# Row maxima of 48 row blocks taken over two key blocks at a time, six maxima per projection task, and projection steps of the attention phase that take only what is over

## The chip, the cores and the metric

The kernel runs on one core of a Trainium2 chip. The metric is the device time of one execution in microseconds (us). TensorE does the matmuls, VectorE (DVE) and ScalarE (ACT) read their results from PSUM, GpSimd (POOL) takes part of the elementwise work, and SyncE (SP) issues most of the DMAs. Each engine has its own queue of instructions.

## The reference

One transformer block over 2048 tokens of 448 features, in fp32, with conditioning vectors made from `c`:

```
mod = silu(c) @ w_mod                       # six vectors: sa, ca, ga, sb, cb, gb
h = layernorm(x) * (1 + ca) + sa
q, k, v = h @ wqkv                          # 16 heads of 28
p = softmax(q k^T / sqrt(28))               # 2048 x 2048 per head
x = x + ga * ((p v) @ wo)
h = layernorm(x) * (1 + cb) + sb
x = x + gb * (gelu(layernorm(h) @ w1 + b1) @ w2 + b2)
```

The softmax needs, for every head and query row, a number near the row's maximum score. The kernel takes that maximum from a first, coarse product of q and k, apart from the exact scores.

## The kernel before

The sequence is cut in four blocks of 512 tokens, the heads in four groups `g` of four, 32 rows each. Every operand of an exact product is split into a high and a low part (`hi`, `lo`), and a product is made of the terms hi x hi, lo x hi and hi x lo.

*First phase (lines 511 to 602).* For each token block, 10 to 14 tasks, 48 in all, numbered here from 0. A q/k task (`qk_task`, line 334) makes q or k of one group for one block: eleven matmuls into a PSUM tile `pa` (two buffers, line 337), then some row maxima, then ScalarE copies the result out (line 352), splits it, and DMAs write both parts to DRAM. A v task (`v_task`, line 363) does the same for v. Between them stand the layer norm of the next block and the transposes of its chunks (`h_chunk`, line 253, in the PSUM tile `o`).

*Row maxima.* The maxima of one head (`j`), one 128-row part (`i`) of a query block (`qt`) over one key block (`cch`) are one unit of work, here "a maximum": a matmul over 32 rows into a PSUM tile `mx` (line 382), and a VectorE reduce over its 512 columns (line 388). Four of them, with different `j`, use different row groups of TensorE. There are 16 for each (g, qt, cch), 1024 in all. They stand in a list `mxq` that is kept sorted, group 1 ahead of group 0 in the first phase, and `emit_max` (line 436) takes the next ones. A task of the first phase takes `p1_n[0]` of them, four in block 0 and five later (`P1RATE`, line 542), with five buffers `mx`.

When the 64 of a (g, qt) are done, `max_fin` (line 398) reduces the four key blocks to one value, and two steps later `put` transposes it (line 404), ScalarE negates it (line 406) and a DMA (line 407) writes it into row 28 of the q tile of that unit, where k has a row of ones: so the score matmul subtracts it. A unit's scores can't start before that DMA has landed. At the end of the first phase `finish_max(0, 0)` and `tick_late(True)` see to it that this is done for unit 0 (lines 600, 601). Then the PSUM pool is closed and the second phase opens its own.

*Second phase (lines 926 to 970).* 16 units (g, qt) of 16 steps, one for each 128 keys. A step makes the scores of four heads in two halves (line 953, twelve matmuls into tiles `s`), ScalarE takes the exponential of each half (line 958), and TensorE multiplies the exponentials of the step before with v (line 919). Between the score matmuls stand three or four maxima of later units, by a budget (lines 942, 943). From unit 12 on, steps 8 to 11 of each unit also make the output projection of a finished block (`t_wo`, line 721, matmuls at line 315): "projection steps". At step 13 of unit 14, when the maxima are done, `share(1, 3)` closes the pool with three `mx` and two `s` buffers and opens one with one and three.

*Third phase.* The MLP.

Of the kernel before, what the change touches and what calls it, by code (L numbers as in the profile page):

```python
# [13 lines left out]
F32 = mybir.dt.float32  # L14
F32R = mybir.dt.float32r
AF = mybir.ActivationFunctionType
ALU = mybir.AluOpType
# [24 lines left out]
def tile_adaln_block(ctx: ExitStack, tc: tile.TileContext, x, wqkv, wo, w1, b1, w2, b2, c, w_mod, out):  # L42
# [20 lines left out]
    def slot(tag, shape, dt=F32R):  # L63
        return sb.tile(shape, dt, tag="slot_" + tag, name=nm("slot_" + tag), bufs=1)
# [17 lines left out]
    def ps_mx():  # L82
        return psp[0].tile([128, 512], F32, tag="mx", name=nm("mx"), bufs=psp[1])
# [7 lines left out]
    def f(t):  # L91
        return t.bitcast(F32)
# [173 lines left out]
        return lambda: split_chunk(k, full, hi, lo, pool, act.copy)  # L266


    sil_b = slot("d0", [CK, NC, 32], F32)
    dve.tensor_copy(sil_b, sil[:, :, None].broadcast_to([CK, NC, 32]))  # L270
    pm = ps_s()
    warm = ps_s()
# [61 lines left out]
    def qk_task(b, kind, g, done=0, begun=None):  # L334
        p, ts = begun or qk_terms(b, kind, g)
        for i in range(done, len(ts)):
            pe.matmul(p, *ts[i], start=(i == 0), stop=(i == len(ts) - 1))  # L337
        emit_max(p1_n[0])
        bias = ones_col if kind == 1 else zero_col
        if g == 0:  # L340
            tg = ("kh" if kind else "qh") + str(b)
            hi = sb.tile([128, 512], F32R, tag=tg, name=nm(tg), bufs=1)
            (kh_sb if kind else qh_sb)[(g, b)] = hi
        elif g == 1 and b < 2:

            hi = sbt("raw" if kind else "osb", [128, 512], F32R, bufs=3 if kind else 2)
            (kh_sb if kind else qh_sb)[(g, b)] = hi
        else:
            hi = sbt("hi", [128, 512], F32R, bufs=3)
        full = sbt("full", [128, 512], bufs=3)  # L350
        lo = sbt("lo", [128, 512], F32R, bufs=3)
        act.activation(full, p, AF.Identity, bias=bias)  # L352

        def split():
            (act.copy if b else dve.tensor_copy)(hi, full)
            pool.tensor_tensor(out=lo, in0=full, in1=f(hi), op=ALU.subtract)
            sl = slice(b * 512, (b + 1) * 512)
            sp.dma_start(f(dscr[kind][0][g])[:, sl], f(hi))
            sp.dma_start(f(dscr[kind][1][g])[:, sl], f(lo))

        return split

    def v_task(b, t):
        p = ps_s()
        ts = slice(t * 128, (t + 1) * 128)
        hh, hl = hT[b]
        mm_acc(p[:, :D], terms448(
            lambda k: hh(k)[:, ts], lambda k: hl(k)[:, ts], lambda k: wv[0][:, k, :], lambda k: wv[1][:, k, :],
        ))
        emit_max(p1_n[0])  # L370
        act.copy(v_sb[b][:, t, :, :DH], p[:, :D].rearrange("p (h d) -> p h d", d=DH))


    mxp = {}
    left = {}
    mxq = []

    def max_one(g, qt, cch, i, j):
        if (g, qt) not in mxp:
            mxp[(g, qt)] = sbt("mxp", [128, 4, 4, 4], bufs=6)  # L380
        m = ps_mx()
        pe.matmul(  # L382
            m,
            qh_sb[(g, qt)][32 * j : 32 * j + 32, i * 128 : (i + 1) * 128],
            kh_sb[(g, cch)][32 * j : 32 * j + 32, :],
            start=True, stop=True,
        )
        dve.tensor_reduce(out=mxp[(g, qt)][:, i, j, cch : cch + 1], in_=m, op=ALU.max, axis=AX.X)  # L388

    def load_hi(kind, g, b):  # L390
        tg = ("kh" if kind else "qh") + str(b)
# [5 lines left out]

    def max_fin(g, qt):
        m16 = sbt("m16", [128, 4, 4], bufs=2)
        dve.tensor_reduce(out=m16, in_=mxp[(g, qt)].rearrange("p i h c -> p h i c"), op=ALU.max, axis=AX.X)  # L400

        def put():
            p = ps_mx()
            pe.transpose(p[:16, :128], m16.rearrange("p h i -> p (h i)"), ident)
            r = sbt("full", [128, 512], F32R, bufs=3)[:16, :128]
            act.activation(r, p[:16, :128], AF.Copy, scale=-1.0)
            sp.dma_start(f(qst[g * NB + qt])[DH:128:32, 0, :].rearrange("j (i q) -> j i q", q=128), f(r))

        late.append([2, put, g * NB + qt])
# [21 lines left out]
    pair_no = {}  # L431


    last_j = [None]

    def emit_max(n, half=None):
        for _ in range(n):
            if not mxq:
                return
            fits = [x for x, m in enumerate(mxq[:32]) if half is None or (m[4] // 2 == half and m[4] != last_j[0])]  # L440
            g, qt, cch, i, j = mxq.pop(fits[0] if fits else 0)
            last_j[0] = j
            max_one(g, qt, cch, i, j)
            left[(g, qt)] -= 1
            pair_no[(g, cch)] = pair_no.get((g, cch), 0) + 1
            if pair_no[(g, cch)] == 16 * NB and g + 1 < NG:
                load_hi(1, g + 1, cch)
            if left[(g, qt)] == 0:
                max_fin(g, qt)
                if g + 1 < NG:  # L450
                    load_hi(0, g + 1, qt)

    p1_n = [0]

    def finish_max(g, qt):
        while left[(g, qt)] > 0:
            emit_max(1)
# [69 lines left out]
    for b in range(NB):  # L527
# [11 lines left out]
        for n, (tb, kind, g) in enumerate(tasks):  # L539
# [2 lines left out]
            p1_n[0] = P1RATE if b < 1 else P1RATE + 1  # L542
            if not more and n == len(tasks) - 1:
                p1_n[0] = 0
            if kind < 2:
                fn = qk_task(tb, kind, g, 6, firsts[n]) if b == 0 and n < 2 else qk_task(tb, kind, g)
                if g == 0:
                    fn()
                else:
                    post.append(fn)  # L550
                if kind == 1 and (g == 0 or (g == 1 and tb < 2)):
                    newq = [(g, qt, cch) for qt in range(tb + 1) for cch in range(tb + 1) if max(qt, cch) == tb]
            else:
                v_task(tb, g)
# [42 lines left out]
                fn()  # L597
        if more:
            stages = later
    finish_max(0, 0)  # L600
    tick_late(True)
    ps1_cm.__exit__(None, None, None)
# [304 lines left out]
        for d, fn in unit_end_tasks(u, o_sb):  # L907
            at(base + 1 + d, fn)

    budget = 0.0  # L910
    pend = None
    o = None
    total_pairs = len(mxq)
    rate = total_pairs / (NKT * (NU - 1) - 6)

    def av(u, kt, p, o):
        g = u // NB
# [8 lines left out]
    for u in range(NU):  # L926
        g, qt = divmod(u, NB)
        for kt in range(NKT):
            step = u * NKT + kt
            if kt == 1 and u + 1 < NU and u + 1 not in qst:  # L930
                load_q(u + 1)
            if kt == NKT - 6 and u + 1 < NU:
                finish_max(*divmod(u + 1, NB))
            tick_late()
            if u == NU - 2 and kt == NKT - 3:
                assert not mxq and not late
                share(1, 3)
            pt = slot(ptags[step % 3], [128, 4, 512], F32)
            budget += rate

            wo_step = u >= NU - NB and 8 <= kt < 12
            n = 3 if wo_step else 4 if (step % 2 == 0 and budget > -4) or budget >= 4 else 3
            n0 = 1 if n == 3 and step % 4 == 3 else 2
            budget -= n

            ks, qs = kst[(g, kt // 4)], qst[u]
            kc = slice((kt % 4) * 128, (kt % 4 + 1) * 128)
            for hf in range(2):
                s2 = ps_s2()
                for term, (kp, qp) in enumerate(((0, 0), (1, 0), (0, 1))):  # L950
                    for jj in range(2):
                        rows_ = slice(64 * hf + 32 * jj, 64 * hf + 32 * jj + 32)
                        pe.matmul(s2[:, jj, :], ks[rows_, kp, kc], qs[rows_, qp, :], start=(term == 0), stop=(term == 2))  # L953
# [4 lines left out]
                act.activation(pt[:, 2 * hf : 2 * hf + 2, :], s2, AF.Exp, scale=SCALE)  # L958
# [102 lines left out]
```

## Time and profile before

| | us |
|---|---|
| median of 3 runs (lowest, highest) | 1161.24 (1160.32, 1162.51) |
| the profiled execution | 1159.49 |
| its span, first to last instruction | 1157.4 |
| first phase: first projection matmul to first score matmul | 20.1 to 184.5 |
| second phase, from there to the last product with v | 184.5 to 859.3 |
| third phase, from there to the end | 859.3 to 1157.4 |

Times inside the trace count from the start of the span. In a row of the timeline stand start, length, engine, line, operation, output and inputs, and how many of them were merged; in brackets how long the engine sat idle before and what it waited for. A row of the windows gives, for a stretch, its length and each engine's busy time and count, then the granted TensorE clock, the DMA share and GB/s. A row of the groups gives busy time, mean ns of one, and the idle time before.

### The profile page before, as it was taken

Reading aid. Unit: us, or ns where it says so; the run is one execution under the profiler, and the core shown is the slowest. Engines: PE = TensorE matmul, PEld = TensorE weight load, DVE = VectorE, ACT = ScalarE, POOL = GpSimd, SP = SyncE. Lnnn points to the kernel's source line nnn. Section 1 sums busy time; section 2 is a strip of 40 time slices with the busy share of each in tenths; the row PEclk is TensorE's granted clock in tenths of the full one; section 3 lists DMA queues with packets and bytes.
Section 4 is the critical chain, followed back from the end, with each engine's and each line's share of the span. In section 5 each row is a group of like instructions: output and inputs, shape, how many; then the busy total and the mean of one; then the engine's idle time right before and its main releaser. Section 6 shows DMA issues by size and latency. Waiting matters only on the chain. (4 is left out here: it accounts for less than half of the span.)

```text
span 1157.4 us, 20604 instructions
## 1 busy us (share of the span) xinstructions
PE 1142.6 (99%) x8396; PEld 685.0 (59%) x8396; DVE 853.7 (74%) x1471; ACT 663.0 (57%) x807; POOL 213.8 (18%) x215
## 2 busy tenths in 40 slices
PE   8999999999999999999999999999999999999998
PEld 6667765444444444444444444545458888888887
DVE  6879888999898889888998877686438863444322
ACT  4644536778777777777777776675863221111110
POOL 2533431210000000000000011206223513223000
PEclk9999999999999999999999999999999999999999
DMA  8652353012131111221120321120323100000000
GB/s 296 201 156 98 108 194 116 29 56 67 48 96 61 56 47 38 84 75 47 50 72 20 83 84 52 34 77 8 109 69 87 50 33 1 1 33 1 32 1 33
DMA packets 50415, 81.07 MB, mean 70 GB/s; under 512 B 11512, under 2 KB 20812, under 8 KB 50320
## 3 DMA queue, kind: packets, MB, share of 16 engines
q1 hardware_dynamic: 49696, 79.01, 21.9%
q8 instruction: 66, 1.08, 0.4%
q10 hardware_dynamic: 288, 0.46, 0.1%
q0 software_dynamic: 336, 0.28, 0.1%
q14 instruction: 29, 0.24, 0.1%
HBM read 53.11 MB, written 26.35 MB: 69 GB/s over the span
## 5 line engine op out<-in xcount | busy, mean ns | idle before, releaser
L388 DVE TENSOR_REDUCE mxp<-mx 128x1 f32<-128x512 f32 x1024 | 640.3, 683 | 100.5 <-PE mx L382 93.2
L953 PE MATMUL s<-slot_b,slot_a 32*128 32x512 f32 x3072 | 380.3, 423 | 2.1 <-ACT slot_d L958 1.0
L958 ACT ACTIVATE slot_c<-s 128x1024 f32<-128x1024 f32 x342 | 331.4, 1022 | 86.5 <-PE s L953 85.1
L953 PEld LDWEIGHTS s<-slot_b,slot_a 32*128 32x128 f32 x3072 | 214.9, 183 | 240.6 <-ACT slot_c L958 138.9
L382 PE MATMUL mx<-kh,qh 32*128 32x512 f32 x960 | 300.5, 472 | 1.2 <-DVE mxp L388 0.2
L958 ACT ACTIVATE slot_d<-s 128x1024 f32<-128x1024 f32 x170 | 164.8, 1021 | 43.4 <-PE s L953 43.4
L919 PE MATMUL o<-slot_c,v 128*32 128x512 f32 x1368 | 183.1, 605 | 0.4 <-ACT osb L905 0.4
L994 ACT ACTIVATE full<-mx,b_col 128x512 f32<-128x512 f32 x56 | 38.5, 688 | 191.9 <-PE mx L315 179.7
L382 PEld LDWEIGHTS mx<-kh,qh 32*128 32x128 f32 x960 | 121.2, 182 | 27.2 <-DVE mxp L388 17.6
L997 DVE CAST hi<-full 128x512 fp32r<-128x512 f32 x56 | 25.2, 450 | 135.4 <-ACT full L994 135.4
L704 POOL TENSOR_TENSOR osb<-osb,osb 128x512 f32<-128x512 f32 x16 | 21.3, 1333 | 485.7 <-DMA osb<-drec 362.2
L919 PE MATMUL o<-slot_d,v 128*32 128x512 f32 x680 | 90.6, 605 | 0.0
L315 PE MATMUL mx<-y,slot_a 128*128 128x512 f32 x160 | 60.6, 395 | 0.0
L919 PEld LDWEIGHTS o<-slot_c,v 128*32 128x32 f32 x1368 | 27.1, 108 | 55.5 <-issue 50.8
L352 ACT ACTIVATE full<-pa,cst 128x512 f32<-128x512 f32 x32 | 22.0, 686 | 52.8 <-PE pa L337 52.8
L998 DVE TENSOR_TENSOR lo<-full,hi 128x512 fp32r<-128x512 f32 x56 | 44.1, 788 | 5.2
L315 PE MATMUL mx<-y,slot_c 128*128 128x512 f32 x152 | 47.5, 396 | 0.1
L1012 PE MATMUL s<-slot_v,lo 128*128 128x448 f32 x128 | 46.7, 365 | 0.0
L1010 PE MATMUL s<-slot_v,hi 128*128 128x448 f32 x128 | 46.6, 364 | 0.0
L315 PE MATMUL mx<-y,slot_v 128*128 128x512 f32 x112 | 39.2, 396 | 0.0
L315 PE MATMUL mx<-y,slot_b 128*128 128x512 f32 x112 | 39.0, 398 | 0.0
L337 PE MATMUL pa<-slot_c,slot_a 128*128 128x512 f32 x136 | 36.9, 405 | 0.0
(212 smaller groups left out, 1289.7 us busy)
## 6 DMA issues: line engine op xcount, KB each, us to landing
d<-lo SPq DMA_DIRECT2D x32, 256.0 KB
slot_b<-d SPq DMA_DIRECT2D x32, 256.0 KB
slot_a<-d SPq DMA_DIRECT2D x32, 256.0 KB
d<-hi SPq DMA_DIRECT2D x20, 256.0 KB
osb<-drec SPq DMA_DIRECT2D x15, 256.0 KB
out_dram<-xn SPq DMA_DIRECT2D x16, 224.0 KB
slot_v<-in_w_mod_dram SPq DMA_DIRECT2D x4, 784.0 KB
raw<-in_B_w_dram SPq DMA_DIRECT2D x14, 224.0 KB
```

The lines of the kernel that those rows point to most:

```text
L315: pe.matmul(p, a, b, start=(i == 0), stop=(i == len(terms) - 1))
L337: pe.matmul(p, *ts[i], start=(i == 0), stop=(i == len(ts) - 1))
L382: pe.matmul(m, qh_sb[(g, qt)][32 * j : 32 * j + 32, i * 128 : (i + 1) * 128], kh_sb[(g, cch)][32 * j : 32 * j + 32, :], start=True, stop=True,
L388: dve.tensor_reduce(out=mxp[(g, qt)][:, i, j, cch : cch + 1], in_=m, op=ALU.max, axis=AX.X)
L919: pe.matmul(o[32 * j : 32 * j + 32, :], v_sb[kt // 4][:, kt % 4, 4 * g + j, :], p[:, j, :], start=(kt == 0), stop=(kt == NKT - 1),)
L953: pe.matmul(s2[:, jj, :], ks[rows_, kp, kc], qs[rows_, qp, :], start=(term == 0), stop=(term == 2))
L958: act.activation(pt[:, 2 * hf : 2 * hf + 2, :], s2, AF.Exp, scale=SCALE)
L994: act.activation(gf, p, AF.Gelu_apprx_tanh, bias=b1_col[:, i : i + 1])
L997: dve.tensor_copy(ghi, gf)
L998: dve.tensor_tensor(out=glo, in0=gf, in1=f(ghi), op=ALU.subtract)
L1010: pe.matmul(pp, ghi[:, ts], w_hi, start=(m == 0), stop=False)
L1012: pe.matmul(pp, glo[:, ts], w_hi, start=False, stop=(m == NFT - 1))
```

## The change

For the three units (0, 1), (0, 2) and (0, 3), the maxima over key blocks 0 and 1 are taken together. With a = q k0 and b = q k1, max(a, b) = a + relu(b - a), and b - a is q (k1 - k0). GpSimd makes the difference of the two k blocks once, `k_diff`. A pair is then two 32-row matmuls: one with `k_diff`, whose result ScalarE passes through a relu into a scratch in the slot `d0`, and one with k0, which VectorE adds to the scratch while it takes the maximum of the sum (`tensor_tensor_reduce`). That is 48 pairs for 96 maxima.

A task of the first phase takes one pair in blocks 0 and 1 and two in blocks 2 and 3 while there are any, puts the pair's first matmuls ahead and its second ones after two single maxima, and picks singles for the row groups that the pairs leave free. Where the tile `o` isn't needed by the task, a sixth matmul goes there.

In the second phase plain steps alternate between four and three maxima, and a projection step takes only what the plain steps left to come can't take at that rate. The pools are changed as soon as no maxima are left.

```diff
-    sil_b = slot("d0", [CK, NC, 32], F32)
+    d0 = slot("d0", [128, 4, 512], F32)
+    sil_b = d0[:CK, 0, 0 : NC * 32].rearrange("p (k r) -> p k r", r=32)
...
-        emit_max(p1_n[0])
+        emit_task(*p1_n)
...
+            if kind == 1 and (g, b) == (0, 1):
+                k_diff.append(sbt("raw", [128, 512], F32R, bufs=3))
+                pool.tensor_tensor(out=k_diff[0], in0=f(hi), in1=f(kh_sb[(0, 0)]), op=ALU.subtract)
...
+    def pair_diff(g, qt, i, j):
+        m = max_mm(g, qt, i, j, k_diff[0])
+        r = d0[:, 2 + px_no[0] % 2]
+        px_no[0] += 1
+        act.activation(r, m, AF.Relu)
+
+        def rest(ps):
+            m = max_mm(g, qt, i, j, kh_sb[(g, 0)], ps)
+            dve.tensor_tensor_reduce(
+                out=r, in0=m, in1=r, scale=1.0, scalar=-3.0e38, op0=ALU.add, op1=ALU.max,
+                accum_out=mxp[(g, qt)][:, i, j, 1:2],
+            )
+
+        return rest
...
+        if (g, qt) in paired and cch < 2:
+            if cch == 1:
+                pxq.extend((g, qt, i, j) for i in range(4) for j in range(4))
+            return
...
+    def emit_task(n, sixth, n_pairs):
+        if not n:
+            return
+        pairs = [pxq.pop(0) for _ in range(min(n_pairs, len(pxq)))]
+        rests = [pair_diff(*m) for m in pairs]
+        js = [m[3] for m in pairs]
+        n_ops = n - len(pairs) + (sixth and len(pairs) > 0)
+        singles = []
+        for x in range(n_ops - len(pairs)):
+            if mxq:
+                free = [j for j in range(4) if j not in js] or range(4)
+                fits = [y for y, m in enumerate(mxq[:32]) if m[4] == free[x % len(free)]]
+                singles.append(mxq.pop(fits[0] if fits else 0))
+        ops = [lambda ps, m=m: max_one(*m, ps) for m in singles]
+        ops[2:2] = rests
+        for x, op in enumerate(ops):
+            op(ps_o if x + len(pairs) == 5 else ps_mx)
...
+            k = n - (5 if b == 1 else 4)
+            p1_n[2] = 1 if b < 2 else 2
+            p1_n[1] = not (more and (0 <= k < NC)) and not (b == 1 and n < 4)
...
+    def is_wo(s_):
+        return s_ // NKT >= NU - NB and 8 <= s_ % NKT < 12
+
+    def left_steps(s_):
+        rest = range(s_, NKT * (NU - 1) - 6)
+        n_wo = sum(is_wo(x) for x in rest)
+        return len(rest) - n_wo, n_wo
+
+    def n_maxima(s_):
+        n_plain, n_wo = left_steps(s_)
+        over = len(mxq) - 7 * n_plain // 2
+        if is_wo(s_):
+            return max(0, -(-over // max(n_wo, 1)))
+        plain[0] += 1
+        return 4 if plain[0] % 2 or (over > 3 * n_wo and over > 0) else 3
...
-            if u == NU - 2 and kt == NKT - 3:
-                assert not mxq and not late
+            if not (three or mxq or late):
+                three = True
                 share(1, 3)
...
-            n = 3 if wo_step else 4 if (step % 2 == 0 and budget > -4) or budget >= 4 else 3
+            n = n_maxima(step)
...
-                    if hf == 0 and term < n0:
+                    if hf == 0 and term < min(n0, n):
                         emit_max(1, 1)
-                    if hf == 1 and (term == 0 or (term == 2 and n - n0 > 1)):
+                    if hf == 1 and ((term == 0 and n - n0 > 0) or (term == 2 and n - n0 > 1)):
                         emit_max(1, 0)
```

More of the change, by code (lines that the diff above doesn't have):

```diff
@@ L369, in v_task @@
         ))
-        emit_max(p1_n[0])
+        emit_task(*p1_n)
         act.copy(v_sb[b][:, t, :, :DH], p[:, :D].rearrange("p (h d) -> p h d", d=DH))
@@ L376, in tile_adaln_block, with max_mm, max_one @@
     mxq = []
-    def max_one(g, qt, cch, i, j):
+    pxq = []
+    k_diff = []
+    paired = ((0, 1), (0, 2), (0, 3))
+    px_no = [0]
+    def max_mm(g, qt, i, j, k, ps=None):
         if (g, qt) not in mxp:
             mxp[(g, qt)] = sbt("mxp", [128, 4, 4, 4], bufs=6)
[L381 to L388, printed above, removed]
+        m = (ps or ps_mx)()
+        js = slice(32 * j, 32 * j + 32)
+        pe.matmul(m, qh_sb[(g, qt)][js, i * 128 : (i + 1) * 128], k[js, :], start=True, stop=True)
+        return m
+    def max_one(g, qt, cch, i, j, ps=None):
+        m = max_mm(g, qt, i, j, kh_sb[(g, cch)], ps)
+        dve.tensor_reduce(out=mxp[(g, qt)][:, i, j, cch : cch + 1], in_=m, op=ALU.max, axis=AX.X)
+    def pair_diff(g, qt, i, j):
[10 more added lines that the diff above has]
+        return rest
     def load_hi(kind, g, b):
@@ L399, in max_fin @@
         m16 = sbt("m16", [128, 4, 4], bufs=2)
-        dve.tensor_reduce(out=m16, in_=mxp[(g, qt)].rearrange("p i h c -> p h i c"), op=ALU.max, axis=AX.X)
+        c0 = 1 if (g, qt) in paired else 0
+        dve.tensor_reduce(out=m16, in_=mxp[(g, qt)][:, :, :, c0:].rearrange("p i h c -> p h i c"), op=ALU.max, axis=AX.X)
         def put():
@@ L431, in tile_adaln_block, with count @@
     pair_no = {}
+    def count(g, qt, cchs):
+        left[(g, qt)] -= len(cchs)
+        for cch in cchs:
+            pair_no[(g, cch)] = pair_no.get((g, cch), 0) + 1
+            if pair_no[(g, cch)] == 16 * NB and g + 1 < NG:
+                load_hi(1, g + 1, cch)
+        if left[(g, qt)] == 0:
+            max_fin(g, qt)
+            if g + 1 < NG:
+                load_hi(0, g + 1, qt)
     last_j = [None]
@@ L443, in emit_max @@
             max_one(g, qt, cch, i, j)
[L444 to L453, printed above, removed]
+            count(g, qt, [cch])
+    def emit_task(n, sixth, n_pairs):
[15 more added lines that the diff above has]
+            op(ps_o if x + len(pairs) == 5 else ps_mx)
+        for g, qt, cch, i, j in singles:
+            count(g, qt, [cch])
+        for g, qt, i, j in pairs:
+            count(g, qt, [0, 1])
+    p1_n = [0, False, 1]
     def finish_max(g, qt):
@@ L599, in tile_adaln_block @@
             stages = later
+    assert not pxq
     finish_max(0, 0)
@@ L908, in end_unit @@
             at(base + 1 + d, fn)
-    budget = 0.0
     pend = None
     o = None
-    total_pairs = len(mxq)
-    rate = total_pairs / (NKT * (NU - 1) - 6)
+    plain = [0]
+    three = False
+    def is_wo(s_):
[11 more added lines that the diff above has]
+        return 4 if plain[0] % 2 or (over > 3 * n_wo and over > 0) else 3
     def av(u, kt, p, o):
@@ L934, in tile_adaln_block @@
             tick_late()
-            if u == NU - 2 and kt == NKT - 3:
-                assert not mxq and not late
+            if not (three or mxq or late):
+                three = True
                 share(1, 3)
             pt = slot(ptags[step % 3], [128, 4, 512], F32)
-            budget += rate
-            wo_step = u >= NU - NB and 8 <= kt < 12
-            n = 3 if wo_step else 4 if (step % 2 == 0 and budget > -4) or budget >= 4 else 3
+            n = n_maxima(step)
             n0 = 1 if n == 3 and step % 4 == 3 else 2
-            budget -= n
             ks, qs = kst[(g, kt // 4)], qst[u]
```

## The prediction

> **What bounds the kernel now.** I read the page first (busy time, costliest groups), then the timeline of one projection task, the windows of the first phase, the timeline of two attention steps, the windows of the steps that carry an output projection, and last the timeline of the seam between the phases.
>
> ```profile
> PE 1142.6 (99%) x8396; PEld 685.0 (59%) x8396; DVE 853.7 (74%) x1471; ACT 663.0 (57%) x807; POOL 213.8 (18%) x215
> L388 DVE TENSOR_REDUCE mxp<-mx 128x1 f32<-128x512 f32 x1024 | 640.3, 683 | 100.5 <-PE mx L382 93.2
> ```
>
> TensorE is in use from end to end and the row maxima are three quarters of VectorE's work. The whole is a string of stages, so each is priced alone. A projection task is eleven matmuls and a group of maxima (each maximum: one 32-row matmul, one reduce):
>
> ```profile
> 160.04 3.08 DVE L388 TENSOR_REDUCE mxp<-mx 128x1 f32<-128x512 f32 x5 [0.31 <-PE mx L382]
> 160.21 1.20 PE L337 MATMUL pa<-slot_c,slot_a 128*128 128x512 f32 x4
> 162.61 0.39 PE L337 MATMUL pa<-slot_c,slot_a2h 128*128 128x512 f32 x1
> 162.93 0.74 PE L382 MATMUL mx<-kh,qh 32*128 32x512 f32 x5
> 163.46 3.08 DVE L388 TENSOR_REDUCE mxp<-mx 128x1 f32<-128x512 f32 x5 [0.34 <-PE mx L382]
> 163.60 2.78 PE L337 MATMUL pa<-slot_c,slot_a 128*128 128x512 f32 x11
> ```
>
> From 160.21 to 163.60 is a task of 3.4 us. Five reduces in a row take 3.08, so one costs 0.60 start to start (683 ns is one alone). VectorE has 0.3 left: TensorE is the bound by a little. Where VectorE has other work, or TensorE waits for a transpose of finished maxima, it turns round:
>
> ```profile
> 96.94:115.22 18.28, 18.16 (x84) 12.08 (x82) 18.01 (x36) 7.30 (x12) 5.47 (x6) 1.00 0.15 58
> 143.14:167.03 23.89, 23.89 (x114) 16.45 (x113) 21.27 (x36) 8.39 (x13) 7.73 (x6) 1.00 0.51 171
> 167.03:181.35 14.32, 13.73 (x68) 9.50 (x67) 13.37 (x24) 5.30 (x10) 3.72 (x6) 1.00 0.81 256
> 142.71 0.18 PEld L382 LDWEIGHTS mx<-kh,qh 32*128 32x128 f32 x1 [0.37 <-DVE mxp L388]
> ```
>
> The columns after the length are PE, PEld, DVE, ACT, POOL. Seven quiet tasks take 23.89 (3.41 each). Tasks 23 to 27 (counted from 0), with layer-norm statistics on VectorE, take 18.28, with VectorE busy 18.01 of it. Tasks 43 to 46, a q/k task and three v tasks, take 14.32; a v task has shorter matmuls (eleven in 2.50 below against 2.78), so 3.41 + 3 x 3.1 = 12.7 would do. In the second phase:
>
> ```profile
> 399.86 0.50 PE L953 MATMUL s<-slot_b,slot_a 32*128 32x512 f32 x2
> 400.43 2.48 DVE L388 TENSOR_REDUCE mxp<-mx 128x1 f32<-128x512 f32 x4 [0.33 <-PE mx L382]
> 402.60 0.50 PE L953 MATMUL s<-slot_b,slot_a 32*128 32x512 f32 x2
> 404.81 0.50 PE L953 MATMUL s<-slot_b,slot_a 32*128 32x512 f32 x2
> ```
>
> The TensorE rows are the starts of three steps. The first step holds four maxima (four reduces, 2.48) and takes 2.74, the second holds three and takes 2.21: a maximum in a plain step costs 0.53.
>
> **The change, part by part.** The order of the built program gives the counts: 201 maxima in the first phase become 229, of which 96 are taken as 48 pairs; 823 in the second become 795.
>
> *First phase.* VectorE's maximum operations fall from 201 to 181: 133 reduces and 48 pair operations. The trace has no pair operation. The nearest row below is a plain two-input operation from PSUM, 686 ns (about 0.60 back to back, if it overlaps as a reduce does); above it twice a reduce, 1.37, if it went over its data twice. The built program holds two instructions a pair, the second writing one column, so I add part of a small instruction (182) and take 0.75.
>
> ```profile
> L803 DVE TENSOR_TENSOR y<-mx,y 128x512 fp32r<-128x512 f32 x12 | 7.9, 686 | 10.6 <-ACT y L801 10.5
> L164 DVE BATCH_NORM_AGGREGATE mv<-st 128x2 f32<-128x6 f32 x48 | 8.7, 182 | 1.6
> L801 ACT CAST y<-mx 128x512 fp32r<-128x512 f32 x13 | 7.3, 589 | 4.4 <-PE mx L240 4.4
> 115.22:136.67 21.45, 21.45 (x114) 15.64 (x113) 18.44 (x31) 13.43 (x24) 11.41 (x11) 1.00 0.45 148
> ```
>
> The Trainium skill ("VectorE: DVE Perf Modes", section on two Vector instructions with no wait between them) says that an operation with an accumulator output is a main instruction and an accumulator read; it gives no price for the read, and no run so far shows one.
>
> A group of six has no more passes over TensorE than one of five, since the order puts at most two in one row group: nothing. Task 13 goes from four to five: +0.2, one matmul of 512 columns. Tasks 23 to 27: 25 reduces (15.0) become 16 reduces and 7 pair operations (9.6 + 5.25 = 14.85), and the last two tasks end with less left on VectorE; between nothing and 0.6, I take -0.3. Task 35: its wait of 0.37 goes, -0.4. Tasks 43 to 46: two reduces and two pairs are 2.7, under 3.1, and the two transposes of finished maxima are no longer there: 12.7 for 14.32, -1.6. The relus are 48 x 0.59 = 28 us of ScalarE. It is fullest in tasks 28 to 33, busy 13.43 of 21.45; with twelve relus, 20.5. That just fits under the matmuls; without that cover it costs up to 0.3 a task, some 2 us. The extra subtraction on GpSimd (1.3, k block 1 less k block 0) stands two tasks ahead of its first reader. Sum **-2.1**.
>
> *The seam.* Unit 0's maxima are now finished after the last task: the order shows nine maxima of (0, 0) after its matmuls, and only then the last reduce, the transpose, the copy and the DMA that carry the maxima into the q tile which the first score matmul reads. Before, that DMA was issued tasks earlier.
>
> ```profile
> 139.58 5.58 DVE L388 TENSOR_REDUCE mxp<-mx 128x1 f32<-128x512 f32 x9 [0.37 <-PE mx L382]
> L400 DVE TENSOR_REDUCE m<-mxp 128x16 f32<-128x64 f32 x16 | 3.5, 220 | 0.6
> 181.32 0.28 PE L404 MATMUL mx<-ident,m 128*16 128x128 f32 x1 [0.27 <-DVE mxp L388]
> 181.35 2.52 PE L315 MATMUL pa<-slot_e,slot_c 128*128 128x448 f32 x11
> 181.69 0.27 ACT L406 ACTIVATE full<-mx 16x128 fp32r<-16x128 f32 x1 [1.02 <-PE mx L404]
> 181.98 0.55 SPq L407 DMA_DIRECT2D slot_b<-full  x1
> 184.49 0.50 PE L953 MATMUL s<-slot_b,slot_a 32*128 32x512 f32 x2 [0.62 <-ACT v L371]
> 818.76 0.55 SPq L689 DMA_DIRECT2D den<-osb  x1
> 820.63 0.25 DVE L695 RECIPROCAL rec<-den 128x16 f32<-128x16 f32 x1 [5.36 <-DMA den<-osb]
> ```
>
> On the clock of this trace: the last projection matmul starts at 183.5 (181.35 + 2.52 - 0.37); the maxima 0.32 later (162.61 to 162.93), VectorE 0.53 after that, 184.35. Nine reduces 5.58: 189.9. Last reduce 0.14 beyond (0.22 less the overlap): 190.1. Transpose to DMA issue 0.66 (181.32 to 181.98): 190.7. An 8 KB DMA from issue to its waiting reader 1.87 (818.76 to 820.63): 192.6. The first scores start there and not at 184.49: **+8.1**. Nothing covers it: no other TensorE instruction stands between in its queue. SP's reload of q for the next group stands ahead of this DMA but waits only for the ninth matmul, some 3.7 earlier.
>
> *Second phase.* Seven of the 28 leave plain steps (one each in units 3, 7 and 10, two each in 12 and 13): 7 x 0.53 = **-3.7**. The other 21 leave projection steps: 7, 8 and 6 in units 12, 13 and 14.
>
> ```profile
> 685.87:703.61 17.74, 3.67 (x12) 1.60 (x12) 1.00 0.00 1
> 734.40:755.08 20.68, 4.28 (x12) 1.96 (x12) 1.00 0.01 2
> 786.46:806.30 19.84, 3.00 (x8) 1.28 (x8) 1.00 0.01 2
> 833.82:852.17 18.35, 0.00 (x0) 0.00 (x0) 1.00 0.34 91
> 836.02 2.62 PE mx L315 x12
> 796.90 1.17 PE L953 MATMUL s<-slot_b,slot_a 32*128 32x512 f32 x12
> 801.74 1.00 PE L953 MATMUL s<-slot_b,slot_a 32*128 32x512 f32 x12
> 809.30 0.98 PE L953 MATMUL s<-slot_b,slot_a 32*128 32x512 f32 x12 [1.02 <-ACT slot_d L958]
> ```
>
> The first four rows are the windows of the four projection steps of units 12 to 15, busy times of the maxima's matmuls alone. Unit 15 has none and takes 18.35; unit 13 has twelve and takes 2.33 more (0.19 each), unit 14 eight and 1.49 more (0.19). Unit 12 projects three parts of four, 4 x 0.66 less (2.62 / 4), and is 2.0 over that (0.17). At 0.185, 21 are **-3.9** (bounds: 0.11, and 0.53 as in a plain step; the lower one because the step from 796.90 to 801.74 has no maximum among its scores and still takes 4.84, 0.25 over unit 15's mean, so that much of 0.58 a step may be unit 15's third score buffer). The change of PSUM pools now comes as soon as maxima are done, two steps earlier, in a projection step whose 2.62 us of matmuls cover the wait of 1.02 for the last exponential: **-0.9**. A transpose of maxima more, unit 1's, falls into this phase: **+0.3** (0.28).
>
> *Sum:* -2.1 + 8.1 - 3.7 - 3.9 - 0.9 + 0.3 = -2.2. The profiled execution took 1159.49 (span 1157.4 and 2.1 around it), so 1157.3 on its clock; it lies 1.75 under the median of the runs, and 1161.24 - 2.2 = **1159.0**.
>
> **Rivals.** *The pair operation is dear* (the slower side). Place: tasks of two pairs, and tasks 23 to 27. Up to 0.9 it is hidden. At x, a v task needs 1.2 + 2x against 3.1 and a q/k task against 3.4; tasks 23 to 27 pay 7 (x - 0.75). At 1.37: 0.55 x 9 q/k, 0.85 x 4 v, 4.3 in tasks 23 to 27 less 1.1 counted twice, 1.2 at the seam where VectorE is late: +13, 1172. It decides from about 1.12, where 4.5 are lost and the change is 2.3 slower than before. For it: no row of such an operation; against: 686 ns for two inputs.
>
> *The clock falls at the seam.*
>
> ```profile
> 1152.00:1154.00 2.00, 0.40 (x3) 0.03 (x1) 1.61 (x3) 0.00 (x0) 0.00 (x0) 1.00 0.59 223
> 1154.00:1157.10 3.10, 0.00 (x0) 0.00 (x0) 0.00 (x0) 0.00 (x0) 0.00 (x0) 1.00 0.40 152
> 1157.20:1157.40 0.20, 0.00 (x0) 0.00 (x0) 0.00 (x0) 0.00 (x0) 0.00 (x0) 0.50 0.00 0
> ```
>
> After the last matmul (1152.4) the granted clock held 4.7 us and then went to 0.50. At the seam the ninth matmul is done near 187.4 and scores start at 192.6: 5.2 without work but for one transpose. If it falls and stays low as long as it held here, 4.7 at half rate lose 2.3: 1161.3. Against: the transpose splits the gap into 2.7 and 2.2. The Trainium skill ("TensorE: Matmul & The Clock Gate", Part 1) has a free-running window of 3.4 us after which an idle array halves its clock; by that rule neither piece alone would do it. The trace's 4.7 agrees with one to two such windows.
>
> *Projection steps hide maxima anyway:* at 0.11 a maximum, -2.3 for -3.9: 1160.6. *VectorE's relief pays more:* a first phase without any wait for VectorE would be 1.2 shorter still in tasks 23 to 27 (18.28 against 3.41 x 4 + 3.1 = 16.7, of which 0.3 is taken above): 1157.8. *Not what it says* is excluded: the order shows 28 maxima moved.
>
> **How the numbers follow.** Forecast as summed, plus or minus 2.5: 0.48. Dear pair 0.22, fallen clock 0.13, hidden maxima 0.09, more relief 0.08. A run of this kernel tells some 0.2% (2.3 us) from no change; the forecast lies on that line, so it is halved, 0.24 faster and 0.24 within. Faster 0.24 + 0.08 = 0.32; within 0.24 + 0.13 + 0.09 = 0.46; slower 0.22. The range goes from 1155.0 (all favourable bounds but the plain-step price) to 1166.0, which takes in a fallen clock and a pair operation up to about 1.15, and leaves 0.2 out.
>
> **What would show it.** Right: the nine reduces at the seam followed by about 2.7 us without VectorE work, scores starting some 6 later than the first-phase tasks alone would have it; tasks 43 to 46 in 12.7; units 12 to 14 shorter by about 2.4, 2.5 and 2.0. Wrong: a pair of VectorE rows over 1.0 together; TensorE waiting for the relu; a granted clock under 1.00 after the seam; projection steps that keep their length.

## The result and the profile after

| | before | after |
|---|---|---|
| median, us (lowest, highest; 17 runs each) | 1161.39 (1159.93, 1164.9) | 1163.79 (1162.92, 1164.7) |
| ratio after / before, 95% interval | | 1.0016, 1.0009 to 1.0024 |
| profiled execution, its span | 1159.49, 1157.4 | 1164.21, 1162.2 |
| mean granted clock of the profiled execution | 1.00 up to the last matmul | 0.994 |

The change makes the kernel 2.4 us slower; 1159.0 was forecast. The windows of the changed kernel show it stage by stage: the first phase, three stretches of it (one with a low clock, tasks 23 to 27, tasks 43 to 46), the seam from the start of the last task to the first score matmul, the spell of low clock behind it, and the second phase. The columns after the length are PE, PEld, DVE, ACT, POOL, then the granted clock, DMA share and GB/s.

```profile
20.50:180.56 160.06, 158.21 (x806) 110.53 (x806) 122.50 (x264) 98.28 (x176) 63.36 (x61) 0.99 0.49 160
35.03:38.44 3.41, 3.41 (x10) 2.67 (x9) 2.10 (x5) 2.15 (x4) 1.42 (x2) 0.50 0.45 172
98.98:116.48 17.50, 17.50 (x88) 12.10 (x86) 16.68 (x40) 9.53 (x18) 5.07 (x5) 1.00 0.16 60
167.88:180.56 12.68, 12.68 (x71) 9.14 (x69) 10.03 (x25) 9.09 (x17) 3.92 (x7) 1.00 0.71 220
180.56:192.10 11.54, 5.74 (x23) 3.30 (x22) 8.14 (x16) 2.18 (x5) 0.00 (x0) 0.85 0.40 139
188.63:198.87 10.24, 6.78 (x40) 3.47 (x40) 5.00 (x9) 4.14 (x5) 3.14 (x4) 0.50 0.30 72
192.10:864.50 672.40, 670.42 (x6114) 311.28 (x6118) 543.25 (x902) 514.80 (x561) 84.94 (x71) 0.99 0.20 60
```

The same stretches of the kernel before:

```profile
20.13:181.35 161.22, 158.58 (x789) 110.59 (x789) 139.59 (x249) 77.29 (x131) 62.09 (x60) 1.00 0.51 165
181.35:184.49 3.14, 2.52 (x14) 1.97 (x14) 2.30 (x4) 0.80 (x2) 0.00 (x0) 1.00 0.28 91
184.49:859.32 674.83, 671.90 (x6141) 310.44 (x6145) 559.08 (x929) 514.88 (x560) 84.54 (x71) 1.00 0.20 60
```

The first phase is 1.2 shorter, although task 5 ran at half clock; the second phase is 2.4 shorter, although it began at half clock; the seam takes 11.54 for 3.14, 8.4 more than before, and that is more than both gains. The timeline of the seam:

```profile
180.56 2.49 PE L317 MATMUL pa<-slot_e,slot_c 128*128 128x448 f32 x11
183.51 5.47 DVE L397 TENSOR_REDUCE mxp<-mx 128x1 f32<-128x512 f32 x9 [0.51 <-PE mx L392]
189.02 0.22 DVE L427 TENSOR_REDUCE m<-mxp 128x16 f32<-128x64 f32 x1
189.29 0.38 PE L431 MATMUL mx<-ident,m 128*16 128x128 f32 x1 [2.75 <-DVE m L427]
189.77 0.27 ACT L433 ACTIVATE full<-mx 16x128 fp32r<-16x128 f32 x1 [6.15 <-PE mx L431]
190.06 0.62 SPq L434 DMA_DIRECT2D slot_b<-full  x1
192.10 0.79 PE L1030 MATMUL s<-slot_b,slot_a 32*128 32x512 f32 x2 [2.43 <-DMA slot_b<-full]
```

It is the chain that the prediction drew: nine reduces, last reduce, transpose, copy, DMA, scores. But the second idle time, 2.43, ends in matmuls at half rate: a pair of score matmuls takes 0.79 where it took 0.50. The clock had fallen already at 188.63, before the transpose at 189.29.

The pair operation and its accumulator read (minimum/median/maximum in ns; the other 13 pair operations read the tile `o` and take 686), and three rows of the timeline, two pairs one behind the other:

```profile
L409 DVE DVE_READ_ACCUMULATOR2_ANT mxp<- x48: 81/83/85, 65.9 to 182.9; 128x1 f32 x48
L409 DVE CUSTOM_DVE_ANT_0 slot_d<-mx,slot_d x35: 679/681/689, 65.3 to 181.7; 128x512 f32<-128x512 f32 x35
```

```profile
178.62 0.68 DVE L409 CUSTOM_DVE_ANT_0 slot_d<-mx,slot_d 128x512 f32<-128x512 f32 x1
179.23 0.08 DVE L409 DVE_READ_ACCUMULATOR2_ANT mxp<- 128x1 f32 x1
179.23 0.69 DVE L409 CUSTOM_DVE_ANT_0 slot_d<-o,slot_d 128x512 f32<-128x512 f32 x1
```

From 178.62 to 179.23 is 0.61: a pair costs VectorE what a plain maximum costs, and the next pair operation starts together with the read of the accumulator.

### The profile page after: what moved, and what is told of

The parts are those of the page before. It is cut to its first block, busy times and chain, and to the rows that moved or that the text cites. A ratio compares the mean times of both kernels' runs of the same rounds, so it can differ in the third digit from the quotient of the medians.

```text
span 1162.2 us, 20728 instructions
## 1 busy us (share of the span) xinstructions
PE 1143.3 (98%) x8396; PEld 685.7 (59%) x8396; DVE 826.7 (71%) x1471; ACT 685.3 (59%) x855; POOL 215.5 (19%) x216
## 5 line engine op out<-in xcount | busy, mean ns | idle before, releaser
L397 DVE TENSOR_REDUCE mxp<-mx 128x1 f32<-128x512 f32 x923 | 582.4, 684 | 128.1 <-PE mx L392 119.2
L1030 PEld LDWEIGHTS s<-slot_b,slot_a 32*128 32x128 f32 x3072 | 217.3, 184 | 243.5 <-ACT slot_c L1035 140.4
L392 PE MATMUL mx<-kh,qh 32*128 32x512 f32 x898 | 294.9, 471 | 0.9 <-DVE mxp L397 0.5
L392 PEld LDWEIGHTS mx<-kh,qh 32*128 32x128 f32 x898 | 118.6, 183 | 12.8 <-DVE mxp L397 6.2
L405 ACT ACTIVATE slot_d<-mx 128x512 f32<-128x512 f32 x48 | 26.8, 595 | 34.1 <-PE mx L392 33.8
```

What stands on the lines that cost most here:

```text
L392: pe.matmul(m, qh_sb[(g, qt)][js, i * 128 : (i + 1) * 128], k[js, :], start=True, stop=True)
```

## The experiments

**1. The seam taken out.** (1, 1) over key block 1 is left to the second phase, and in the last block the tasks take pairs so that unit 0 is finished at task 42. To this end the singles of unit 0 are picked first once its last key block is there, the scratch gets a third buffer, and the second phase picks its maxima from one group at a time.

```diff
+            fits = [x for x, m in enumerate(mxq[:32]) if m[0] == mxq[0][0] and (half is None or (m[4] // 2 == half and m[4] != last_j[0]))]
...
+                if (0, 0, 3) in queued and mxq[0][:2] == (0, 0):
+                    fits = [y for y in fits if mxq[y][:2] == (0, 0)]
...
+    SKIP = ((1, 1, 1),)
...
-            p1_n[2] = 1 if b < 2 else 2
+            p1_n[2] = 1 if b < 2 or (not more and n < 5) else 2 if more else 3
...
-                    newq = [(g, qt, cch) for qt in range(tb + 1) for cch in range(tb + 1) if max(qt, cch) == tb]
+                    newq = [(g, qt, cch) for qt in range(tb + 1) for cch in range(tb + 1) if max(qt, cch) == tb and (g, qt, cch) not in SKIP]
...
-        r = d0[:, 2 + px_no[0] % 2]
+        r = d0[:, 1 + px_no[0] % 3]
```

> The changed kernel, with unit 0's maxima finished four tasks before the end of the first phase instead of after its last task: the 16 maxima of (1, 1) over key block 1 are left to the second phase (their nine or so net places cost there what a maximum costs in a projection step), the tasks 39 to 42 take one pair and four singles, the tasks 43 to 46 three pairs. Nothing of the computation is left out. Theory (the loss lies at the seam: 8.4 us of chain after the last task, and 2.1 us of half clock in the first two steps behind it): first scores start some 8 us earlier against the last task, the granted clock stays at 1.00 there, nine more maxima in projection steps give back 0.8 to 1.7, so 9 to 10 us under the changed kernel, near 1154. Rival (the chain at the seam only shows time that the second phase would wait for anyway, for the first exponentials or for k and q tiles): the gap to the first scores shrinks by less than 3 and the time stays over 1160.

Measured: 1155.72 (1154.44 to 1157.31), 0.9941 of the kernel before (0.9927 to 0.9954). The windows of its last task and second phase, and of the stretch at half clock:

```profile
179.92:183.05 3.13, 2.51 (x14) 1.99 (x13) 1.92 (x6) 2.29 (x5) 0.00 (x0) 1.00 0.90 298
183.05:857.66 674.61, 672.58 (x6123) 311.27 (x6127) 548.31 (x911) 514.89 (x561) 84.47 (x71) 0.99 0.20 60
185.79:192.61 6.82, 6.82 (x40) 2.70 (x39) 4.33 (x8) 3.69 (x5) 3.07 (x4) 0.50 0.29 70
```

The seam is back at 3.13, as before the change. Against the changed kernel the gain is 8.1 by the two medians (8.7 by the two ratios to the kernel before), for 9 to 10 expected. What is missing lies with the clock: it fell here too in the profiled execution, though TensorE had no gap over 0.62 at this place, and of the six runs the two with a mean clock of 0.999 took 1154.44 and 1154.54, the two with 0.997 1157.08 and 1157.31. So the seam is the loss, and the clock is a matter by itself.

**2. Idle matmuls that keep the clock up.**

```diff
     finish_max(0, 0)
+    warm = ps_s()
+    for _ in range(11):
+        pe.matmul(warm[:, :128], ident, ident, start=True, stop=True)
     tick_late(True)
+    for _ in range(10):
+        pe.matmul(warm[:, :128], ident, ident, start=True, stop=True)
```

> The changed kernel with 21 idle 128-column matmuls at the seam, 11 behind the last maximum of unit 0 and 10 behind the transpose, whose results nobody reads. The chain at the seam keeps its length. Theory (the fall of the clock to 0.50 after the gap of 5.2 us is a loss of its own, 2.06 us in the steps 0 and 1 of unit 0): the granted clock stays at 1.00 at the seam, these two steps take 2.1 and 2.8 again, and the time is 2 us under the changed kernel, 1161.7. Rival (the two steps are slow because the first exponentials or the score buffers are late, and the clock in the record is only beside it): clock or not, the steps stay at 2.8 and 4.2 and the time stays within 0.5 of the changed kernel.

Measured: 1162.81 (1161.13 to 1167.78), 1.0007 of the kernel before (0.9994 to 1.002). The timeline: the first scores stand at 192.10 as in the changed kernel, but take 0.49; the windows are the seam and the steps 0 and 1 of unit 0.

```profile
186.62 2.72 PE L667 MATMUL pa<-ident 128*128 128x128 f32 x22
189.55 2.40 PE L670 MATMUL pa<-ident 128*128 128x128 f32 x20
192.10 0.49 PE L1035 MATMUL s<-slot_b,slot_a 32*128 32x512 f32 x2 [0.16 <-PE pa L670]
```

```profile
186.00:192.10 6.10, 5.74 (x45) 5.07 (x45) 3.34 (x7) 0.27 (x1) 0.00 (x0) 1.00 0.20 50
192.10:194.20 2.10, 1.71 (x16) 0.92 (x16) 1.49 (x3) 1.05 (x2) 0.00 (x0) 1.00 0.46 123
194.20:197.00 2.80, 2.78 (x23) 1.13 (x23) 2.79 (x5) 2.65 (x3) 1.51 (x2) 1.00 0.20 46
```

The two steps in the changed kernel:

```profile
192.10:194.91 2.81, 2.44 (x16) 1.51 (x16) 1.90 (x4) 1.07 (x2) 0.96 (x1) 0.50 0.50 117
194.91:199.10 4.19, 4.19 (x23) 1.85 (x23) 2.52 (x4) 2.80 (x3) 2.18 (x4) 0.53 0.34 74
```

7.00 against 4.90: the fall costs 2.1, and the theory holds at its place. The median moved by 1.0 only. The profiled execution lost 1.6 at a late DMA in unit 5 (41.65 for 40.04) and 0.7 in unit 15, and other runs go up to 1167.78, so the median does not show the whole 2.1.

**3. The old rule of the second phase.**

```diff
-            n = n_maxima(step)
+            budget += rate
+            wo_step = u >= NU - NB and 8 <= kt < 12
+            n = 3 if wo_step else 4 if (step % 2 == 0 and budget > -4) or budget >= 4 else 3
...
+            budget -= n
```

> The changed kernel with the second phase's old budget rule, so three maxima in each projection step (instead of one or so) and correspondingly fewer plain steps with four. Counted in the program's order: 20 plain steps fewer with four, 21 maxima more in projection steps; the first phase and the seam are as in the changed kernel. Theory (a fourth maximum costs 0.53 in a plain step and one in a projection step 0.09): -20 x 0.53 + 21 x 0.09 = -8.7, 1155. Rival (a maximum costs 0.185 in a projection step, as the prediction had it): -10.6 + 3.9 = -6.7, 1157. Second rival (0.53 is only the price of a step with four among neighbours with four, and three after three brings nothing): no change, 1163 to 1164.

Measured: 1163.53 (1163.06 to 1164.56), 1.0012 of the kernel before (1.0002 to 1.0022). My theory and the first rival fall; the second rival holds. The counts on which the expectation stood were too high: against the changed kernel the trace has 13 plain steps that went from four to three (not 20) and 13 maxima more in projection steps (not 21), namely 15 more in units 12 and 13 and two fewer in unit 14. With these counts the theory gives -5.7 and the first rival -4.5, and both still fall. The maxima in the projection steps of units 12 and 13, first in the changed kernel (after the length the busy time and count of the maxima's matmuls), then here:

```profile
694.81:712.05 17.24, 1.99 (x5) 0.73 (x5) 1.00 0.01 1
742.03:761.66 19.63, 1.97 (x4) 0.72 (x4) 1.00 0.00 1
792.21:812.36 20.15, 0.78 (x2) 0.37 (x2) 1.00 0.01 2
```

```profile
694.33:712.00 17.67, 3.67 (x14) 1.60 (x12) 1.00 0.01 1
741.45:762.26 20.81, 4.61 (x12) 1.97 (x12) 1.00 0.01 1
```

Fifteen maxima more in these eight steps cost 0.43 + 1.18 = 1.61, 0.11 each. (Two of the fourteen records of the first row lie at its edge; the order has twelve.) And the 13 plain steps that went from four to three brought nothing: unit 8, with two of them, took 40.03 for 40.10, unit 5, also with two, 40.05 for 40.04. The starts of the products with v, one a step, in unit 6, where the three steps before 452.99 carry three maxima each:

```profile
445.74 1.06 PE L1002 MATMUL o<-slot_c,v 128*32 128x512 f32 x8
448.03 1.06 PE L1002 MATMUL o<-slot_c,v 128*32 128x512 f32 x8
450.69 1.07 PE L1002 MATMUL o<-slot_d,v 128*32 128x512 f32 x8
452.99 1.07 PE L1002 MATMUL o<-slot_c,v 128*32 128x512 f32 x8
```

Steps of 2.29, 2.66, 2.30: the last two take 4.96, as two steps with four and three do.

**4. Six maxima in each projection step**, on top of experiment 1; the plain steps take what is left (`rate`), three, three and four in turn.

```diff
+    WO = 6
+    plain = [0.0]
...
         if is_wo(s_):
-            return max(0, -(-over // max(n_wo, 1)))
...
+            return WO
...
+        plain[0] += rate
+        n = 4 if plain[0] >= 3.5 else 3
...
-            n0 = 1 if n == 3 and step % 4 == 3 else 2
+            n0 = 3 if n > 4 else 1 if n == 3 and step % 4 == 3 else 2
```

> The kernel of the early seam, with six maxima in each projection step and so few in the plain steps (three, four in one of three) that the units' maxima are still ready in time. Against the early seam alone, whose projection steps take two, some 36 plain steps go from four maxima to three, and 40 maxima more stand in projection steps. Theory (any maximum that goes from a plain step's fourth place into a projection step gains 0.53 less 0.09 to 0.19): -36 x 0.53 + 40 x 0.09 to 0.19 = -12 to -15 against the early seam, near 1141. Rival (only the first three or so of a step find free places between other matmuls, and the fourth to sixth cost 0.5 there too): -19 + 10 x 0.1 + 30 x 0.5 = -3, near 1151.

Measured: 1194.59 (1193.36 to 1195.58), 1.027 of the kernel before (1.0255 to 1.0285); both expectations are missed by far, on the slow side. In the plain units 4 to 10 three steps took 7.69 (2.74, 2.74, 2.21): more time for fewer maxima. Of some 39 us over experiment 1, the profiles show 14 in units 0 to 11 and 24 in units 12 to 14. The four projection steps of unit 12 took 26.92; this is what TensorE's weight loads (PEld) waited for in them, in us in total, times, and the longest:

```profile
PEld mx L392 <- DVE mxp L397: 5.9, 14, 0.6
PEld mx L317 <- DVE mxp L397: 4.2, 4, 1.7
```

Both the maxima and the projection itself (line 317, whose output stands in the same `mx` buffers) wait for VectorE to give a buffer back. Six a step are no longer hidden there. What each costs can't be read from this: spells of half clock lie in these windows too (718.62 to 722.04 in unit 12).

**5. The seam alone, in the kernel before.** Nine maxima of unit 0 are held back; no pairs, old rule.

```diff
+        if (g, qt, cch) == (0, 0, 0):
+            held.extend(mxq[-9:])
+            del mxq[-9:]
...
+    mxq[:0] = held
     finish_max(0, 0)
```

> The kernel before with one thing alone: nine of unit 0's maxima (of key block 0) are held back until after the last task of the first phase, as the change brought it about. Everything else, pairs and rule included, is as before; the tasks 9 to 11 lose the nine. Theory (the seam's chain is exposed in full, and the clock falls behind it in every run): first scores 8.4 later after the last task's start, steps 0 and 1 of unit 0 longer by 2, tasks 9 to 11 shorter by nothing to 1: 8 to 10.5 over the kernel before. Rival (the seam is dear only together with the pairs, whose relus and reduces crowd VectorE and ScalarE at the end of the phase): under 4 over the kernel before.

Measured: 1169.78 (1168.81 to 1171.72), 1.0077 of the kernel before (1.0063 to 1.009): 9.3 more, inside the theory's range. The windows of the seam and of the steps behind it:

```profile
181.89:193.42 11.53, 5.54 (x23) 3.10 (x23) 8.00 (x14) 1.07 (x3) 0.00 (x0) 0.80 0.16 50
193.42:202.49 9.07, 8.71 (x55) 4.82 (x55) 5.46 (x9) 4.10 (x5) 3.09 (x4) 0.50 0.40 99
```

11.53 for 3.14, with no pair in the program. With experiment 1 this settles the seam from both sides.

**6 and 7. A fuller step 0**, in the kernel before and in that of experiment 1.

```diff
             pend = (u, kt, pt, o)
+            if step == 0:
+                for j in range(4):
+                    pe.matmul(o[32 * j : 32 * j + 32, :], v_sb[0][:, 0, j, :], f(kh_sb[(0, 0)]), start=True, stop=True)
```

> The kernel before with four 32-column-group matmuls more in step 0 of unit 0, in the place where every other step has its product with v (their result is overwritten). Theory (the runs of the kernel before scatter over 6 us because the clock falls to 0.50 for one to three spells of 3.4 us at thin places, the start of the second phase being one, where step 0 has only 32-row matmuls): the runs with a mean granted clock under 0.998 become rarer and the median falls by 0.5 to 1.5 less up to 0.5 for the matmuls. Rival (the falls lie elsewhere, in the first tasks of the first phase): same scatter, and 0 to 0.5 slower.

> The kernel of the early seam with the same four matmuls in step 0. In the profile of the early seam the granted clock fell to 0.50 from 185.79 to 192.61, right behind step 0, though TensorE had no gap there over 0.62. Theory (step 0 without a product with v is too thin for the clock): the clock stays at 1.00, steps 1 and 2 take 2.8 and 2.75 instead of 4.36 and 3.67, 2 us under the early seam in a run that has that fall, 1 us in the median: 1154.5. Rival (the fall there comes of the 0.62 gap and the layout of the weights, which the four matmuls don't change): clock 0.50 again at that place, no gain.

Measured: 1160.44 (1159.39 to 1161.76) beside 1160.49 (1160.06 to 1162.73) for the kernel before, 0.9997 (0.9988 to 1.0006); and 1156.33 (1155.07 to 1157.88), 0.9959 (0.9946 to 0.9972). In experiment 7's profile the clock stayed at 1.00 at the seam and steps 1 and 2 took 2.18 and 2.73, as the theory says, with 2.77 for 2.14 in step 0: unit 0 took 39.84 for 42.28 in the profile of experiment 1. But the median is 1.8 over the 1154.5 expected and no better than that of experiment 1. In experiment 6 no run had a mean clock under 0.998, where 5 of the 15 runs of the kernel before beside it had, down to 0.995; its median is the same, against the theory. The four matmuls themselves cost nothing there: steps 0 and 1 took 2.77 and 2.18 for 2.13 and 2.80. So the fall can be held off in this way, but no median shows a gain from it, and why it doesn't is not settled.

**8. The same number of fours, in another order.**

```diff
-        return 4 if plain[0] % 2 or (over > 3 * n_wo and over > 0) else 3
+        return 4 if plain[0] % 4 in (1, 2) or (over > 3 * n_wo and over > 0) else 3
```

> The changed kernel with the same number of maxima in the plain steps, but in the order 4, 4, 3, 3 instead of 4, 3, 4, 3; projection steps and all else unchanged. Theory, formed on the runs so far (a plain step takes one of two times, 2.21 or 2.74; it takes 2.21 only behind a step of 2.74 and with three maxima at most, so a fourth maximum is free in every second step and costs 0.53 in the others): a group of four steps takes 2.74 + 2.74 + 2.21 + 2.74 = 10.43 instead of 9.90, 0.53 more in 55 groups: 29 over the changed kernel, about 1192. Rival (a fourth maximum has a price of its own, 0.53 wherever it stands, as the prediction used it): no change, 1163 to 1165.

Measured: 1187.29 (1186.75 to 1188.49), 1.0225 of the kernel before (1.0206 to 1.0244), 23.5 over the changed kernel. The products with v in unit 8, and one of the waits between them:

```profile
535.44 1.06 PE L1000 MATMUL o<-slot_c,v 128*32 128x512 f32 x8
538.18 1.07 PE L1000 MATMUL o<-slot_c,v 128*32 128x512 f32 x8
540.93 1.07 PE L1000 MATMUL o<-slot_d,v 128*32 128x512 f32 x8
543.67 1.06 PE L1000 MATMUL o<-slot_c,v 128*32 128x512 f32 x8
545.88 1.07 PE L1000 MATMUL o<-slot_c,v 128*32 128x512 f32 x8
```

```profile
543.24 0.18 PEld L392 LDWEIGHTS mx<-kh,qh 32*128 32x128 f32 x1 [0.48 <-DVE mxp L397]
```

2.74, 2.75, 2.74, 2.21, as the theory has it. The sum is smaller, 23.5 for 29, since a unit has only three such groups at their full price (41.92 for 40.06 on average in units 1 to 11): the group with the transpose of finished maxima was slow anyway. The rival falls. In a slow step the last maximum's weights wait 0.48 for VectorE to free one of three buffers. Why a step with three maxima is slow too when it stands behind a fast one is not settled.

**9. The rule alone, in the kernel before.** The `n_maxima` of the change in place of the budget; nothing else.

> The kernel before with the second phase's new rule alone: no pairs, five maxima a task, 823 in the second phase. Counted in the program's order: the surplus goes to the start, unit 0 has four maxima in all its steps and unit 1 in one more, and units 3, 7, 10, 12 and 13 lose their extra fours; projection steps keep three. Theory (only fours in every second step cost): 9 x 0.53 more in units 0 and 1, 7 x 0.53 less later, 0.5 less by the earlier change of pools: +0.6 over the kernel before, within what can be told from no change. Rival (the rule is what brings the second phase's gain, by itself): 3 to 4 under the kernel before.

Measured: 1162.39 (1160.67 to 1164.63), 1.0013 of the kernel before (1.0003 to 1.0023), so 1.5 slower where 0.6 was expected. The profile has two falls of the clock that the profile of before lacks, one from 34.93 to 38.34 in the first phase and one in step 1 of unit 0 (4.07 for 2.80). The rival falls: the rule by itself brings nothing.

## Why the prediction was wrong

By its own steps, on the traces of the two kernels:

- *First phase, -2.1.* -2.7: 160.06 less 161.22 is -1.16, and task 5 took 5.13 for 3.60 at half clock, before the first pair; experiments 1, 4 and 7 run the same program there without a fall. Tasks 23 to 27 take 17.50 for 18.28 (-0.8, forecast -0.3; a pair costs 0.61 and not 0.75), tasks 43 to 46 12.68 for 14.32 (-1.6 as forecast), task 13 +0.2 as forecast and task 35 -0.3 (forecast -0.4). The relus were hidden: from 60 to 183 no gap of TensorE is over 0.25.
- *Seam, +8.1.* +8.4, and experiments 1 and 5 show it from both sides. Right.
- *Plain steps, -3.7.* -3.6 in units 3, 7, 10, 12 and 13. Right, but for a narrower reason than was given: these seven were fours in the second place of a pair of steps. A fourth maximum in the first place is free (experiment 3), so 0.53 isn't the price of a maximum but of being at the wrong place (experiment 8).
- *Projection steps, -3.9.* **This step failed.** The three windows went from 17.74, 20.68 and 19.84 to 17.24, 19.63 and 20.15. Of the last, 0.59 belongs to the change of pools (5.43 for 4.84 in the step where TensorE waited 0.72 for ScalarE to copy the last transposed maxima out of the old pool); then it is -0.50, -1.05 and -0.28, together -1.8 for 21 maxima, 0.087 each in place of 0.185; experiment 3 gives 0.11. The rival "projection steps hide maxima anyway" is what happened, with a price under its 0.11. The 0.185 came of comparing with unit 15, which has three score buffers where the others have two; that the buffers make the difference is likely, but no run changes them alone.
- *Change of pools, -0.9.* -0.3: it saved 0.92 in the last four steps of unit 14 and cost 0.59 in a projection step. The cover of 2.62 us of matmuls that I named did not hide this wait.
- *The transpose, +0.3.* +0.3 in unit 0; but the transposes of the other units moved as well, and beyond the terms above units 2 and 10 to 14 took some 0.2 to 0.4 more each, units 1, 3, 6 and 7 some 0.15 to 0.3 less: about +1 that the sum didn't have.
- *"The clock falls at the seam", put at 0.13 as a rival and at nothing in the sum.* It fell, in the profile for 10.24 us, and cost 2.1 (experiment 2). All 17 runs of the changed kernel have a mean clock of 0.992 to 0.995. **This was the second step that failed:** the argument against it was that the transpose splits the gap in two pieces too short for a fall; but the clock fell at 188.63, inside the first piece, 2.1 us after the last maximum's matmul had ended and before the transpose at 189.29.
- *The dear pair operation, 0.22.* Excluded by its rows: 0.61 back to back.
- *From which run the sum was counted.* The profiled execution of before had no fall of the clock ahead of its last matmul; most of the others have some. In 55 runs of before, those with a mean clock of 1.000 averaged 1159.96 (11 runs), those with 0.997 1162.71 (11) and those with 0.995 1164.28 (5). So the profile compares +4.8 in span, and the medians +2.4.

On the profiles: -2.7 + 1.5 + 8.4 + 2.1 - 3.6 - 1.8 - 0.3 + 0.3 + 1.0, with +0.4 before the first task and -0.4 in the third phase, is +4.9, for +4.8 measured. The seam's chain was foreseen and is larger than the whole loss: with unit 0 finished earlier (experiment 1) the change gains 6.4 us, the fastest kernel of this study. The sign was missed mainly by two terms of about 2 us each, the maxima in projection steps and the clock, in a sum of terms that nearly cancel.

## What to carry to other kernels

When work is postponed, look first at what becomes last at the next stage boundary: nine cheap operations behind the last task laid open a serial chain of 8.4 us, more than the rest of the change saved all over the kernel (some 7 us in the profiles). A price per operation read from two neighbouring steps holds only for that place in the cycle; before it is multiplied, look for a stretch where the same operation stands in the other place, or try it there. And a sum that starts from one profiled execution should say which events of chance (here, spells of low clock) that execution had or lacked.

## What was not expected of the hardware

The granted clock falls to 0.50 without any long gap, and the spells in these profiles last 3.41, 6.83, 10.24 or 13.65 us, one to four times 3.41. If the profiles are cut into stretches of 3.41 us on the edges of those spells, these are the stretches (here "windows") ahead of a fall: in the changed kernel at the seam and at task 4, and in experiment 1 at the start of the second phase.

```profile
185.22:188.63 3.41, 1.12 (x3) 0.36 (x2) 3.41 (x7) 0.00 (x0) 0.00 (x0) 1.00 0.22 56
31.62:35.03 3.41, 2.07 (x13) 0.99 (x12) 2.12 (x5) 3.41 (x8) 1.63 (x2) 1.00 0.77 264
```

```profile
182.38:185.79 3.41, 2.35 (x25) 1.36 (x24) 2.14 (x4) 2.21 (x3) 0.02 (x1) 1.00 0.64 185
```

And the same place in experiment 7, where no fall followed:

```profile
182.10:185.51 3.41, 2.77 (x28) 1.18 (x30) 2.30 (x4) 2.29 (x3) 0.00 (x0) 1.00 0.00 0
```

That looks like a threshold of busy time between 2.35 and 2.77, but three more windows speak against it. In experiment 1 the window at task 4, as busy as that of the changed kernel, is followed by no fall; in experiment 3 (second row) and experiment 4 (third row) falls follow windows that are busier than that of experiment 7.

```profile
32.19:35.60 3.41, 2.07 (x12) 1.27 (x9) 2.76 (x6) 3.41 (x8) 1.27 (x1) 1.00 0.75 259
181.68:185.09 3.41, 2.89 (x13) 1.45 (x11) 2.90 (x8) 0.53 (x1) 0.00 (x0) 1.00 0.60 215
773.24:776.65 3.41, 3.03 (x20) 1.19 (x21) 3.38 (x7) 1.77 (x3) 1.13 (x1) 1.00 0.00 0
```

So the time for which TensorE is busy in a window does not decide by itself whether the clock falls: in the eleven profiles of this case, falls ahead of the last matmul followed windows busy between 1.12 and 3.03 us. What does decide is not shown here. The Trainium skill ("TensorE: Matmul & The Clock Gate", Part 1) has a free-running window of 3.4 us, which these lengths agree with, and a fall after an idle one; here windows that were busy for two thirds and more were enough. A two-input operation with an accumulator takes 681 ns and its accumulator read 83 ns, and two of them in a row start 0.61 apart, so the read adds nothing there.
